# gate_w as SyncE's first transfer, and the gate's product on 16 partitions

## The chip, the core and the metric

One core of a Trainium2 chip runs the whole program. The metric is the device time of one execution in microseconds; a comparison takes the median of several runs. A profile is taken of one execution, and times within it count from the first instruction of the program (the span's start).

## The reference

A decode step for two rows x (2 x 1 x 512, bf16). Branch A is attention over a cache of 4096 keys and values for 32 heads of 128; branch B is a small ReLU network; a sigmoid gate mixes them.

```python
x = A_x                                                   # [2, 1, 512]
g = sigmoid((x * gate_w).sum(-1, keepdims=True))          # gate_w: [512]
q = (x @ wq).reshape(2, 1, 32, 128).transpose(0, 2, 1, 3)
s = einsum("bhqd,bhkd->bhqk", q, k_cache) * 128 ** -0.5   # k_cache: [2, 32, 4096, 128]
a = einsum("bhqk,bhkd->bhqd", softmax(s), v_cache)
a = a.transpose(0, 2, 1, 3).reshape(2, 1, 4096) @ wo
b = relu(x @ w1) @ w2                                     # w1: [512, 1376]
out = g * a + (1 - g) * b
```

The gate needs, for each of the two rows, one dot product of 512 elements; everything else hangs on reading the two caches, 67 MB each.

## The kernel before

The program is written as a list of instructions per engine with semaphores between them; each engine runs its list in order. SyncE's queue (sp) carries all large loads, in this order: wq (L218), w1 (L219), then sixteen units of 8 MB, eight of the K cache and eight of the V cache (L231; the last V unit in two parts, L226 and L228), then wo (L236) and w2 (L239 to L242), and at the end the output (L243). The order of the units is k0 to k4, then v0, k5, v1, k6, v2, k7, v3 to v7. They share three regions of SBUF (kv, three times 64 KB per partition). A unit is loaded when the unit three places earlier has been used up. wq and w1 lie in the third region, C, so the third unit, k2, waits for the q and h products and for the setup (L224). In the same region lie the small things of the beginning: x, gate_w, an identity and a block of ones.

ScalarE's queue carries two small loads: x as two rows of 1 KB (L216) and gate_w as one row of 1 KB (L217).

What the engines do in the first 20 us:

- GpSimd fills constants (constants(), L249 to L263).
- gate() (L280): TensorE transposes x to 128 partitions, four columns of two (L282, waits for x), and gate_w likewise (L285, waits for gate_w). VectorE copies the results out of PSUM (xT L287, a padded copy xT32 L289, gwT L291), multiplies x by gate_w on 128 partitions (L292), sums over the four columns (L294), and TensorE sums over the partitions with the block of ones (L296). ScalarE takes the exponential (L298); VectorE finishes the sigmoid after setup().
- setup() (L266): six small VectorE operations on the identity, masks for later. They stand in VectorE's list between the gate's sum and its sigmoid.
- q_proj() (L308): 32 products of TensorE (L313), which wait for wq and xT, then a VectorE transpose and a copy (L320, L323).
- ffn_h() (L327): 44 small products (L334), which wait for w1; VectorE applies ReLU and 1 - g (L338, L341).

Then, per K unit, VectorE transposes the unit in four pieces in place (k_turn, L358) and TensorE forms the scores (L363 and L391). A softmax runs per batch row (L397 to L420). Per V unit GpSimd spreads the probabilities (L429), TensorE multiplies (L446), VectorE extracts the diagonal blocks (L453, L457) and TensorE gathers them (L462). The end is project(): the products with wo and w2 (L499) into one PSUM tile, a copy (L505) and the output. The gate's value g is used first in the h branch (gm, 1 - g, L338) and then when the attention's result is scaled.

Of the kernel before, what the change touches and what calls it, by code (L numbers as in the profile page):

```python
# [4 lines left out]
ALU = mybir.AluOpType  # L5
ACT = mybir.ActivationFunctionType
AX = mybir.AxisListType
# [77 lines left out]
def bass_gated_mix__gqa_block_cached__dense_activation_relu__decode_kernel(  # L85
# [13 lines left out]
    bf16, f32 = dt.bfloat16, dt.float32  # L99

    sb = nc.alloc_sbuf_tensor
    kv = sb("kv", [128, NREG, REG], bf16)
# [5 lines left out]
    id2 = sb("id2", [2, 2], bf16)  # L108
    xT = sb("xT", [128, 4, 2], bf16)
    xT32 = sb("xT32", [128, 4, 32], bf16)  # L110
    gwT = sb("gwT", [128, 4], bf16)
    xg = sb("xg", [128, 4, 2], f32)
    xgs = sb("xgs", [128, 2], f32)
    ez = sb("ez", [128, 2], f32)
    ez1 = sb("ez1", [128, 2], f32)
    gb = sb("gb", [128, 2], f32)
# [23 lines left out]
    C = NREG - 1  # L140
    wq_sb = kv[:, C, 0:16384]
    w1_sb = kv[:, C, 16384:21888]
    x_sb = kv[0:2, C, 21888:22400]
    gw_sb = kv[0:1, C, 22400:22912]
    ident = kv[:, C, 22912:23168].bitcast(f32)
    ones = kv[:, C, 23168:23424].bitcast(f32)

    PSF = nc.alloc_psum_tensor("PS", [128, 4096], f32)
    PSB = PSF[:, :].bitcast(bf16)
# [6 lines left out]
    G_C0 = MISC + 64  # L156
    H_C0 = 7 * BANK + 400
    L_C0 = MISC + 96
    XT_B0 = 2 * (MISC + 400)

    def psf(p0, p1, c0, n):
        return PSF[p0:p1, c0:c0 + n]

    for e in ("pe", "dve", "act", "pool"):
        P.sems[e] = nc.alloc_semaphore(e + "_ev")
    names = ["x", "gw", "wq", "w1", "v7a", "v7b", "wo0", "wo1", "wo2", "w2a", "w2e", "w2b", "w2c", "w2d", "out"]
    sem = {n: nc.alloc_semaphore("sem_" + n) for n in names}
    sem_reg = [nc.alloc_semaphore(f"sem_reg{s}") for s in range(NREG)]

# [13 lines left out]
    def freed(what):  # L183
        kind, u = what
        return f"pe_sc_{u}" if kind == "k" else f"pe_v_{u}"

    def sp(fn, waits=(), dwaits=()):
        P.add("sp", fn, waits=waits, dwaits=dwaits)
# [4 lines left out]
    def dve(fn, waits=(), signal=None, dwaits=()):  # L193
        P.add("dve", fn, waits=waits, signal=signal, dwaits=dwaits)

    def act(fn, waits=(), signal=None, dwaits=()):
        P.add("act", fn, waits=waits, signal=signal, dwaits=dwaits)

    def pe(fn, waits=(), signal=None, dwaits=()):
        P.add("pe", fn, waits=waits, signal=signal, dwaits=dwaits)  # L200
# [13 lines left out]
    w2_sb = kv[:, WO, 16384:22016].rearrange("p (r n) -> p r n", n=512)  # L214

    act(lambda e: e.dma_start(x_sb, A_x.rearrange("b s d -> (b s) d")).then_inc(sem["x"], 16))  # L216
    act(lambda e: e.dma_start(gw_sb, gate_w.rearrange("(o d) -> o d", o=1)).then_inc(sem["gw"], 16))  # L217
    sp(lambda e: e.dma_start(wq_sb, A_wq.rearrange("(p t) n -> p (t n)", t=4)).then_inc(sem["wq"], 16))  # L218
    sp(lambda e: e.dma_start(w1_sb, B_w1.rearrange("(p t) f -> p (t f)", t=4)).then_inc(sem["w1"], 16))  # L219
    for n, what in enumerate(order):  # L220
        if n >= NREG:
            waits = [freed(order[n - NREG])]
        else:
            waits = ["pe_h", "dve_setup", "dve_q"] if n == C else []  # L224
# [5 lines left out]
        else:  # L230
            sp(lambda e, n=n, what=what: e.dma_start(kv[:, n % NREG, :], unit_in(what)).then_inc(sem_reg[n % NREG], 16),  # L231
               waits=waits)
# [8 lines left out]
    for name, r0, r1 in (("w2b", 0, 5), ("w2c", 5, 9), ("w2d", 9, 10)):  # L241
        sp(lambda e, name=name, r0=r0, r1=r1: e.dma_start(w2_sb[:, r0:r1, :], w2_in[:, r0:r1, :]).then_inc(sem[name], 16))  # L242
    sp(lambda e: e.dma_start(out.rearrange("b s (t n) -> t (b s) n", n=128), out_sb[0:128:16, :]).then_inc(sem["out"], 16),  # L243
       waits=["dve_out"])
# [21 lines left out]
    def setup():  # L266
        dve(lambda v: v.tensor_reduce(out=maskc[:], in_=ident.rearrange("p (t c h) -> p c t h", t=4, c=4), axis=AX.XY, op=ALU.add),
            waits=["c_ident"])
        dve(lambda v: v.tensor_reduce(out=mmax[:], in_=ident.rearrange("p (h x) -> p h x", h=8), axis=AX.X, op=ALU.add),
            signal="dve_m8")  # L270
        dve(lambda v: v.tensor_copy(out=mask8[:], in_=mmax[:]), waits=["dve_m8"], signal="dve_mask8")
        dve(lambda v: v.tensor_reduce(out=selx[:, 24:32], in_=ident.rearrange("p (y h) -> p h y", h=8), axis=AX.X, op=ALU.add),
            waits=["c_selx"], signal="dve_selx")
        for h in range(2):
            dve(lambda v, h=h: v.tensor_reduce(
                out=sell[:, h, :].rearrange("p (u a e) -> p e u a", u=4, a=4)[:, h],
                in_=ident.rearrange("p (a u r e) -> p e u a r", a=4, u=4, r=4)[:, h], axis=AX.X, op=ALU.add),
                waits=["c_sell"], signal=("dve_setup" if h == 1 else None))

    def gate():  # L280
        for t in range(4):
            pe(lambda e, t=t: e.transpose(PSB[0:128, XT_B0 + 2 * t:XT_B0 + 2 * t + 2], x_sb[:, t::4], id2[0:2, 0:2]),  # L282
               waits=(["c_id2"] if t == 0 else []), dwaits=([(sem["x"], 16)] if t == 0 else []))
        for t in range(4):
            pe(lambda e, t=t: e.transpose(PSB[0:128, XT_B0 + 8 + 2 * t:XT_B0 + 9 + 2 * t], gw_sb[:, t::4], id2[0:1, 0:1]),  # L285
               dwaits=([(sem["gw"], 16)] if t == 0 else []), signal=("pe_xT" if t == 3 else None))
        dve(lambda v: v.tensor_copy(out=xT[:], in_=PSB[0:128, XT_B0:XT_B0 + 8].rearrange("p (t b) -> p t b", t=4)),  # L287
            waits=["pe_xT"], signal="dve_xT0")
        dve(lambda v: v.tensor_copy(out=xT32[:, :, 0:2], in_=PSB[0:128, XT_B0:XT_B0 + 8].rearrange("p (t b) -> p t b", t=4)),  # L289
            waits=["c_x32"], signal="dve_x32")  # L290
        dve(lambda v: v.tensor_copy(out=gwT[:], in_=PSB[0:128, XT_B0 + 8:XT_B0 + 16:2]), signal="dve_xT")  # L291
        dve(lambda v: v.tensor_tensor(out=xg[:], in0=xT[:], in1=gwT[:].unsqueeze(2).to_broadcast([128, 4, 2]), op=ALU.mult),  # L292
            waits=["dve_xT"], signal="dve_xg")
        dve(lambda v: v.tensor_reduce(out=xgs[:], in_=xg[:].rearrange("p t b -> p b t"), axis=AX.X, op=ALU.add),  # L294
            waits=["dve_xg"], signal="dve_xgs")
        pe(lambda e: e.matmul(psf(0, 128, G_C0, 2), lhsT=ones, rhs=xgs[:, :], start=True, stop=True),  # L296
           waits=["dve_xgs", "c_ones"], signal="pe_z")
        act(lambda a: a.activation(out=ez[:], in_=psf(0, 128, G_C0, 2), func=ACT.Exp, scale=-1.0), waits=["pe_z"], signal="act_ez")  # L298
        setup()
        dve(lambda v: v.tensor_scalar(out=ez1[:], in0=ez[:], scalar1=1.0, scalar2=None, op0=ALU.add),  # L300
            waits=["act_ez"], signal="dve_ez1")
        dve(lambda v: v.reciprocal(out=gb[:], in_=ez1[:]), waits=["dve_ez1"], signal="dve_g")
        dve(lambda v: v.tensor_scalar(out=gm[:], in0=gb[:], scalar1=-1.0, scalar2=1.0, op0=ALU.mult, op1=ALU.add),
            waits=["dve_g"], signal="dve_gm")
# [202 lines left out]

    constants()
    gate()
    q_proj()  # L510
    w_block(0)
# [69 lines left out]
```

## Time and profile before

| | |
|---|---|
| median of 3 runs | 345.81 us (345.68 to 345.89) |
| the profiled execution, its own time | 345.56 us |
| its span | 344.24 us (344.2 on the page) |
| busy: TensorE products, VectorE, GpSimd, ScalarE | 53%, 49%, 10%, 4% of the span |
| SyncE's DMA queue, share of sixteen engines' time | 98.2% |
| read from HBM | 145.43 MB, 422 GB/s over the span |
| mean granted TensorE clock | 0.772 |
| x on TensorE, gate_w on TensorE, wq on TensorE | from 2.47, 7.99 and 13.14 us |

The page's slices cut the span into forty pieces of 8.6 us; a digit is the busy share in tenths. In a timeline line the first number is the start, the second the duration (from the first to the last instruction where several are merged), then engine, line of the kernel, operation, what is written and read, the count, and in brackets the idle time before with what ended it. A q behind an engine's name marks its sequencer issuing a DMA; the duration is that of the issue, not of the transfer. The packet records behind the DMA view hold, for each packet of a DMA engine, its start, duration, size and queue; q1 is SyncE's queue and q10 is ScalarE's.

### The profile page before, as it was taken

To read this page: it belongs to the slowest core of one execution; us is meant where nothing else is said; L and a number is where in the kernel's file an instruction comes from. 1 tells how busy PE (TensorE), PEld (TensorE's weight loads), DVE (VectorE), ACT (ScalarE), POOL (GpSimd) and SP (SyncE) were. 2 spreads that over 40 slices of the span, in tenths; PEclk is the share of its full clock that TensorE was granted. 3 is DMA by queue.
4 is the path that set the end of the run, shared out by engine and by line. 5 is a ranking of instruction groups with operands and counts; after the bars stand their busy time and mean duration, and the time that the engine had idled before them with its cause. 6 is when DMAs were issued, how large, how long until landed. Compare 5 with 4: busy or idle time off the path is not lost.

```text
span 344.2 us, 2542 instructions
## 1 busy us (share of the span) xinstructions
PE 182.1 (53%) x1322; PEld 40.5 (12%) x938; DVE 169.5 (49%) x86; ACT 12.9 (4%) x42; POOL 36.1 (10%) x50
## 2 busy tenths in 40 slices
PE   0520197996968409936970199206970604215453
PEld 0220000100100001110120002000120201102232
DVE  0210697979899489439810693119844010101020
ACT  1010001000010210100000000000020000000000
POOL 3000000000000040040022000400004040404000
PEclk9965579898999957995995589856995675856585
DMA  8998999999898999989899999999999999999994
GB/s 328 446 482 373 480 404 449 442 411 487 366 487 375 472 419 434 472 375 487 381 472 389 465 421 426 465 396 472 398 449 411 444 442 411 472 417 413 396 413 176
DMA packets 3744, 145.60 MB, mean 423 GB/s; under 512 B 434, under 2 KB 661, under 8 KB 917
## 3 DMA queue, kind: packets, MB, share of 16 engines
q1 hardware_dynamic: 3727, 145.43, 98.2%
q8 instruction: 9, 0.15, 0.2%
q14 instruction: 2, 0.02, 0.0%
q10 hardware_dynamic: 6, 0.00, 0.0%
HBM read 145.43 MB, written 0.00 MB: 422 GB/s over the span
## 4 chain that ended last, share of the span: by engine, by line
DMA 57%; DVE 20%; PE 13%; issue 4%; another core or an unknown queue 3%; SPq 1%; ACT 1%
DMA kv<-in_A_k_cache_dram 33%; DVE kv L358 18%; DMA kv<-in_B_w_dram 13%; DMA kv<-in_A_v_cache_dram 11%; PE PS L363 7%; PE PS L446 4%; PE PS L391 3%; DVE E L420 1%; ACT E L412 1%; DVE mpad L397 1%; SPq L236 0%; DVE X L457 0%; PE PS L499 0%; DVE X L453 0%
## 5 line engine op out<-in xcount | busy, mean ns | idle before, releaser
L358 DVE STREAM_TRANSPOSE kv<-kv 128x4096 uint32<-128x4096 uint32 x32 | 139.3, 4412 | 49.2 <-DMA kv<-in_A_k_cache_dram 49.2
L363 PE MATMUL PS<-kv,wz 128*128 128x512 bf16 x384 | 115.3, 411 | 0.0
L391 PE MATMUL PS<-kv,wz 128*128 128x512 bf16 x128 | 53.4, 417 | 92.3 <-DVE kv L358 92.3
L429 POOL TENSOR_TENSOR ptm<-E,mask 128x512 bf16<-128x512 bf16 x32 | 32.2, 1039 | 282.1 <-DVE E L420 158.6
L446 PE MATMUL PS<-kv,ptm 128*32 128x512 bf16 x512 | 38.4, 460 | 36.5 <-DMA kv<-in_A_v_cache_dram 36.5
L453 DVE TENSOR_TENSOR X<-PS,maskc 128x512 f32<-128x512 f32 x8 | 5.5, 686 | 79.3 <-PE PS L446 79.3
L391 PEld LDWEIGHTS PS<-kv,wz 128*128 128x128 bf16 x128 | 13.2, 103 | 205.0 <-DVE kv L358 116.6
L446 PEld LDWEIGHTS PS<-kv,ptm 128*32 128x32 bf16 x512 | 17.4, 113 | 54.4 <-issue 47.3
L349 ACT ACTIVATE wz<-q_sb 32x8 bf16<-32x8 bf16 x32 | 6.9, 215 | 154.2 <-PE PS L363 145.4
L462 PE MATMUL PS<-X,selx 128*32 128x128 f32 x16 | 3.5, 302 | 13.2 <-DVE X L457 13.2
L457 DVE TENSOR_REDUCE X<-X 128x128 f32<-128x512 f32 x8 | 8.2, 1024 | 0.3
L397 DVE TENSOR_REDUCE mpad<-PS 128x2 f32<-128x2048 f32 x2 | 4.6, 2292 | 7.5 <-PE PS L363 7.5
L412 ACT ACTIVATE E<-PS,negm 128x1024 bf16<-128x1024 f32 x4 | 4.4, 1108 | 81.9 <-DVE negm L408 81.9
L420 DVE STREAM_TRANSPOSE E<-E 128x2048 bf16<-128x2048 bf16 x2 | 4.6, 2311 | 4.7 <-ACT E L412 4.7
L313 PE MATMUL PS<-kv,xT 128*32 128x512 bf16 x32 | 3.6, 628 | 3.5 <-DMA kv<-in_A_wq_dram 3.5
L499 PE MATMUL PS<-kv,wz 128*17 128x128 bf16 x128 | 3.1, 264 | 3.8 <-DMA kv<-in_A_wo_dram 3.8
L505 DVE CAST ptm<-PS 128x128 bf16<-128x128 f32 x1 | 0.3, 292 | 9.5 <-PE PS L499 9.5
L320 DVE STREAM_TRANSPOSE ptm<-PS 128x1024 f32<-128x1024 f32 x1 | 1.2, 1250 | 6.2 <-PE PS L313 6.2
L287 DVE COPY xT<-PS 128x8 bf16<-128x8 bf16 x1 | 0.2, 162 | 8.3 <-PE PS L285 8.3
L462 PEld LDWEIGHTS PS<-X,selx 128*32 128x32 f32 x16 | 1.1, 112 | 18.9 <-DVE X L457 15.7
L285 PE MATMUL PS<-id,kv 1*128 1x1 bf16 x4 | 0.3, 172 | 5.3 <-DMA kv<-in_gate_w_dram 5.3
L499 PEld LDWEIGHTS PS<-kv,wz 128*17 128x17 bf16 x128 | 2.4, 109 | 4.3 <-DMA kv<-in_A_wo_dram 3.7
(57 smaller groups left out, 26.9 us busy)
## 6 DMA issues: line engine op xcount, KB each, us to landing
kv<-in_A_v_cache_dram SPq DMA_DIRECT2D x1, 6144.0 KB, 47.9
kv<-in_A_wq_dram SPq DMA_DIRECT2D x1, 4096.0 KB, 12.3
kv<-in_A_v_cache_dram SPq DMA_DIRECT2D x1, 2048.0 KB, 52.4
kv<-in_A_wo_dram SPq DMA_DIRECT2D x1, 2048.0 KB, 37.7
kv<-in_A_wo_dram SPq DMA_DIRECT2D x2, 1024.0 KB, 41.1
kv<-in_B_w_dram SPq DMA_DIRECT2D x1, 1376.0 KB, 15.1
kv<-in_B_w_dram SPq DMA_DIRECT2D x1, 640.0 KB, 42.9
kv<-in_B_w_dram SPq DMA_DIRECT2D x1, 512.0 KB, 43.7
```

What stands on the lines that cost most here:

```text
L349: act(lambda e, a=a: e.activation(out=wz[32 * a:32 * a + 32, u % 2, :, 31 + 32 * a:33 + 32 * a], in_=q_sb[32 * a:32 * a + 32, b, ub].rearr ...
L358: dve(lambda v, rp=rp: v.transpose(out=reg[:, 4096 * rp:4096 * (rp + 1)], in_=reg[:, 4096 * rp:4096 * (rp + 1)]), dwaits=([landed(what)] i ...
L363: return e.add_instruction(mybir.InstMatmult(name=nc.get_next_instruction_name(), engine=mybir.EngineType.PE, ins=[e.lower_ap(rhs), e.lowe ...
L391: return e.matmul(dst, lhsT=w, rhs=m, start=first, stop=final, skip_group_check=True)
L397: dve(lambda v: v.tensor_reduce(out=mpad[:, 0:2], in_=PSF[:, 0:2048].rearrange("p (x h q) -> p h x q", h=2, q=16), axis=AX.XY, op=ALU.max) ...
L412: act(lambda a, h=h: a.activation(out=E[:].rearrange("p (x h q) -> p h x q", h=2, q=16)[:, h], in_=PSF[:, 0:2048].rearrange("p (x h q) -> ...
L420: dve(lambda v: v.transpose(out=E[:], in_=E[:]), waits=[f"act_exp{b}"], signal=f"dve_et{b}")
L429: pool(lambda g, src=src, dst=dst: g.tensor_tensor(out=dst, in0=src, in1=msk, op=ALU.mult), waits=([f"dve_et{b}", "dve_mask8"] + ([f"pe_v_ ...
L446: pe(lambda e, ci=ci, t=t: e.matmul(psf(32 * t, 32 * t + 32, c0, 512), lhsT=ptm[:, ci].rearrange("p c h -> p (c h)"), rhs=rows[:, 512 * ci ...
L453: dve(lambda e: e.tensor_tensor(out=X2[:].rearrange("p (c d) -> p c d", c=4), in0=psf(0, 128, c0, 512).rearrange("p (c d) -> p c d", c=4), ...
L457: dve(lambda e: e.tensor_reduce(out=X3[:], in_=X2[:].rearrange("p (c d) -> p d c", c=4), axis=AX.X, op=ALU.add), waits=[f"dve_x_{v}"] + ([ ...
L499: pe(lambda e, t=t, n=n, w=w, m=m: e.matmul(psf(32 * t, 32 * t + 17, FIN_C0, 128), lhsT=w, rhs=m[:, 128 * t:128 * t + 128], start=(n == 0) ...
```

## The change

gate_w leaves ScalarE's queue and becomes the first transfer on SyncE's, ahead of wq, as 16 rows of 32 elements (64 bytes) on 16 partitions. ScalarE's second load becomes x16: x a second time, laid out on the same 16 partitions, 32 elements of each batch row on each. VectorE multiplies them there (16 partitions by 2 x 32) and sums over the 32; TensorE's sum with ones now runs over 16 partitions. The four transposes of gate_w and its copy out of PSUM are gone, and the transposes of x alone release the copies of x. The order of VectorE's list is otherwise kept. The new tiles lie in region C where gate_w's row was.

```diff
-    gwT = sb("gwT", [128, 4], bf16)
-    xg = sb("xg", [128, 4, 2], f32)
-    xgs = sb("xgs", [128, 2], f32)
+    xgs = sb("xgs", [16, 2], f32)
...
-    gw_sb = kv[0:1, C, 22400:22912]
+    x16 = kv[0:16, C, 22400:22464].rearrange("p (b c) -> p b c", b=2)
+    gw16 = kv[0:16, C, 22464:22496]
+    xg = kv[0:16, C, 22496:22624].bitcast(f32).rearrange("p (b c) -> p b c", b=2)
...
     act(lambda e: e.dma_start(x_sb, A_x.rearrange("b s d -> (b s) d")).then_inc(sem["x"], 16))
-    act(lambda e: e.dma_start(gw_sb, gate_w.rearrange("(o d) -> o d", o=1)).then_inc(sem["gw"], 16))
+    act(lambda e: e.dma_start(x16, A_x.rearrange("b s (r c) -> r (b s) c", c=32)).then_inc(sem["x16"], 16))
+    sp(lambda e: e.dma_start(gw16, gate_w.rearrange("(r c) -> r c", c=32)).then_inc(sem["gw"], 16))
     sp(lambda e: e.dma_start(wq_sb, A_wq.rearrange("(p t) n -> p (t n)", t=4)).then_inc(sem["wq"], 16))
     sp(lambda e: e.dma_start(w1_sb, B_w1.rearrange("(p t) f -> p (t f)", t=4)).then_inc(sem["w1"], 16))
...
     def gate():
         for t in range(4):
             pe(lambda e, t=t: e.transpose(PSB[0:128, XT_B0 + 2 * t:XT_B0 + 2 * t + 2], x_sb[:, t::4], id2[0:2, 0:2]),
-               waits=(["c_id2"] if t == 0 else []), dwaits=([(sem["x"], 16)] if t == 0 else []))
-        for t in range(4):
-            pe(lambda e, t=t: e.transpose(PSB[0:128, XT_B0 + 8 + 2 * t:XT_B0 + 9 + 2 * t], gw_sb[:, t::4], id2[0:1, 0:1]),
-               dwaits=([(sem["gw"], 16)] if t == 0 else []), signal=("pe_xT" if t == 3 else None))
+               waits=(["c_id2"] if t == 0 else []), dwaits=([(sem["x"], 16)] if t == 0 else []),
+               signal=("pe_xT" if t == 3 else None))
...
-        dve(lambda v: v.tensor_copy(out=gwT[:], in_=PSB[0:128, XT_B0 + 8:XT_B0 + 16:2]), signal="dve_xT")
-        dve(lambda v: v.tensor_tensor(out=xg[:], in0=xT[:], in1=gwT[:].unsqueeze(2).to_broadcast([128, 4, 2]), op=ALU.mult),
-            waits=["dve_xT"], signal="dve_xg")
-        dve(lambda v: v.tensor_reduce(out=xgs[:], in_=xg[:].rearrange("p t b -> p b t"), axis=AX.X, op=ALU.add),
-            waits=["dve_xg"], signal="dve_xgs")
-        pe(lambda e: e.matmul(psf(0, 128, G_C0, 2), lhsT=ones, rhs=xgs[:, :], start=True, stop=True),
+        dve(lambda v: v.tensor_tensor(out=xg, in0=x16, in1=gw16.unsqueeze(1).to_broadcast([16, 2, 32]), op=ALU.mult),
+            dwaits=[(sem["gw"], 16), (sem["x16"], 16)], signal="dve_xg")
+        dve(lambda v: v.tensor_reduce(out=xgs[:], in_=xg, axis=AX.X, op=ALU.add), waits=["dve_xg"], signal="dve_xgs")
+        pe(lambda e: e.matmul(psf(0, 128, G_C0, 2), lhsT=ones[0:16], rhs=xgs[:, :], start=True, stop=True),
            waits=["dve_xgs", "c_ones"], signal="pe_z")
```

More of the change, by code (lines that the diff above doesn't have):

```diff
@@ L165, in bass_gated_mix__gqa_block_cached__dense_activation_relu__decode_kernel @@
         P.sems[e] = nc.alloc_semaphore(e + "_ev")
-    names = ["x", "gw", "wq", "w1", "v7a", "v7b", "wo0", "wo1", "wo2", "w2a", "w2e", "w2b", "w2c", "w2d", "out"]
+    names = ["x", "gw", "x16", "wq", "w1", "v7a", "v7b", "wo0", "wo1", "wo2", "w2a", "w2e", "w2b", "w2c", "w2d", "out"]
     sem = {n: nc.alloc_semaphore("sem_" + n) for n in names}
```

## The prediction

> **What bounds the kernel now.** I read the page first, its slices and its queue table, then the DMA view of the stretch from 2 to 338 us, then the timeline at both ends, then the chain of waits and SyncE's own issues.
>
> From the page:
>
> ```profile
> span 344.2 us, 2542 instructions
> ...
> DMA  8998999999898999989899999999999999999994
> GB/s 328 446 482 373 480 404 449 442 411 487 366 487 375 472 419 434 472 375 487 381 472 389 465 421 426 465 396 472 398 449 411 444 442 411 472 417 413 396 413 176
> ...
> q1 hardware_dynamic: 3727, 145.43, 98.2%
> ```
>
> No compute engine is over 53% busy, but SyncE's queue (q1) fills 98.2% of the time of the sixteen DMA engines. The DMA view without the first 2 and the last 6 us:
>
> ```profile
> DMA packets 3421, 144.50 MB, mean 430 GB/s; under 512 B 380, under 2 KB 477, under 8 KB 608
> ...
> q1 hardware_dynamic: 3409, 144.36, 99.7%
> ```
>
> Between 2 and 338 us the engines are never without work. The trace's packet records say it more sharply: in every microsecond of that stretch more than 15 packets are in flight in the mean. So what the chain of waits names (33% K loads, 18% DVE transposes) is not the bound in the sense that a faster DVE would help: the loads are issued early enough. The time is: start of the stream, plus a fixed sum of packets, plus the tail behind the last one. The start and the tail:
>
> ```profile
> 0.73 0.54 ACTq L216 DMA_DIRECT2D kv<-in_A_x_dram  x1
> ...
> 0.74 0.39 SPq L218 DMA_DIRECT2D kv<-in_A_wq_dram  x1
> ...
> 1.18 0.42 SPq L219 DMA_DIRECT2D kv<-in_B_w_dram  x1
> 1.30 0.23 ACTq L217 DMA_DIRECT2D kv<-in_gate_w_dram  x1
> ...
> 2.47 0.26 PE L282 MATMUL PS<-id,kv 2*128 2x2 bf16 x4 [2.47 <-DMA kv<-in_A_x_dram]
> ...
> 7.99 0.29 PE L285 MATMUL PS<-id,kv 1*128 1x1 bf16 x4 [5.26 <-DMA kv<-in_gate_w_dram]
> ...
> 9.07 0.59 PE L296 MATMUL PS<-xgs,kv 128*128 128x2 f32 x2 [0.79 <-DVE xgs L294]
> ...
> 13.14 3.60 PE L313 MATMUL PS<-kv,xT 128*32 128x512 bf16 x32 [3.49 <-DMA kv<-in_A_wq_dram]
> ```
>
> ```profile
> 340.97 0.71 PE L499 MATMUL PS<-kv,hT 128*17 128x128 bf16 x20 [0.53 <-DMA kv<-in_B_w_dram]
> 341.73 0.29 DVE L505 CAST ptm<-PS 128x128 bf16<-128x128 f32 x1 [9.47 <-PE PS L499]
> 342.05 0.65 SPq L243 DMA_DIRECT2D out_dram<-ptm  x1
> ```
>
> To be seen here: SyncE's first instruction is the load of wq (0.74); by the packet records its first packet starts at 1.756, 1.02 us after the issue began. The last w2 packet ends at 340.80, and 0.71 + 0.29 + 0.65 us with small gaps and the output's way out follow. What happens on the compute engines at 3 to 13 us stands beside the stream.
>
> **The change, part by part.**
>
> *1. SyncE issues one more transfer ahead of wq.* SyncE starts at 0.74 as before, but with gate_w; wq, w1, k0 and k1 come one issue later. Rows for an issue on SyncE:
>
> ```profile
> 0.74 0.39 SPq L218 DMA_DIRECT2D kv<-in_A_wq_dram  x1
> ...
> 296.47 0.28 SPq L240 DMA_DIRECT2D kv<-in_B_w_dram  x1
> ```
>
> L240 has 8 rows (0.28), L218 128 rows (0.39), most loads of L231 (128 rows) take 0.33, and the first issue on ScalarE (L216, 2 rows) takes 0.54. Between issues lie 0.04 to 0.05. For 16 rows I take 0.33 + 0.05 = 0.38 us, with 0.28 + 0.04 = 0.32 and 0.54 + 0.05 = 0.59 as ends. Nothing hides it: until the first wq packet the engines are empty, and later there is no idle time to absorb it. **+0.38.**
>
> *2. More small packets.* Removed: gate_w as one row of 1 KB, which took 46 ns on one of the sixteen engines, with a 4-byte semaphore packet of 9. Added: 16 rows of 64 B on SyncE and 32 rows of 64 B (16 partitions, two batches) on ScalarE, plus their semaphore packets; spread evenly, an engine gets one and two rows. The gate_w row comes into an empty engine inside the 0.38 us just charged, so it costs nothing there; should wq start at once, it costs its own duration. No 64-byte packet is in the trace. Nearest are the 256-byte rows of the output, 15 to 18 ns, and the 1 KB rows in a busy stream, 46. For x16 I take 2 x 15 + 9 = 39 ns per engine, with 2 x 46 + 9 = 101 above and nothing below. **+0.04.** The far upper end is the first x packet, 1 KB in 366 ns; it is rival C.
>
> *3. wq's slow first packets.* The first packet of wq on each engine took 1.51 to 2.18 us, 1.885 in the mean, where later 32 KB packets take 1.213: 0.67 us per engine is lost. After the change a 64-byte row of gate_w comes first on each engine. If it uses up this cost, wq gets it back: between 0 and -0.67. The nearest rows: the first x packet took 366 ns where 1 KB otherwise takes 46, so about 0.32 is the price of an isolated read. But an isolated 16 KB instruction load at 340.9 us, when the engines have gone empty again, took 958 ns where 16 KB in the stream takes 612: 0.35 late in the program too. So it is more a price of each start from empty than a one-time one, and between gate_w (1.756 + 0.37 = 2.12) and wq (1.756 + 0.38 = 2.14) the engine runs empty again. I take **0**, by the 16 KB row, and keep -0.67 for the range.
>
> *4. The gate's arithmetic.* Four PE transposes (L285, 0.29 together) and one DVE copy (L291, 0.15) go; product and sum stay at one instruction each (0.17 and 0.16) and now wait for x16 and gate_w. The xT copy need no longer wait for gate_w: it moves from 8.32 to about 2.8. x16 takes the old place of gate_w on ScalarE's queue, and that row, issued at 1.30, reached an engine only at 6.35 (some four 32 KB packets of 1.21 stood ahead) and its semaphore packet another packet later, at 7.60. With two rows per engine I expect x16 at 8.8 to 10, so the DVE product starts up to 1.4 us later than the 8.65 of now. What is queued behind it: on DVE the setup reductions (1.2 us) and three small operations, done by about 12; on PE the L296 product, and behind it q_proj (L313), which waits for wq until 13.1 + 0.4 anyway. **0**, covered by wq's own landing with some 2 us to spare.
>
> *5. If that cover were gone.* A late q_proj would move L320 to L341 and the issue of k2 (it waits for the h product, setup and q; it went out at 19.4). But k2's first packets start only at 53.98, behind k0 and k1: 34 us of cover. Of the later loads v1 has least: issued 145.23, its packets begin at 150.71, 5.5 us of cover. All of these come from compute that follows landings, so they slide along with the stream and no new gap opens. DVE itself has room ahead of k0:
>
> ```profile
> 37.08 8.77 DVE L358 STREAM_TRANSPOSE kv<-kv 128x4096 uint32<-128x4096 uint32 x2 [17.07 <-DMA kv<-in_A_k_cache_dram]
> ```
>
> It stands idle for 17.07 us until k0 lands, then two of the transposes run; k0 lands later by what the stream is late.
>
> **Sum:** +0.38 + 0.04 + 0 + 0 = +0.42 us. The profiled execution took 345.56 us, 1.32 outside its span of 344.24; it becomes 344.66 and 345.98. The median of the runs shown is 345.81, 0.25 above the profiled one; the same step on it gives 346.23, which I round to **346.2 us** (+0.12%).
>
> **The rivals.**
>
> *A, the forecast (60%).* The stream starts one issue later and keeps its length. For it: the 98.2%, and no idle slice that could absorb a shift. With the ends of steps 1 and 2: 0.32 + 0 = +0.32 to 0.59 + 0.10 = +0.69, so 346.1 to 346.5.
>
> *B, the small transfer takes the cold start (25%).* gate_w's rows wake the engines, and wq's first packets run at 1.213. All 0.67 spared: 0.42 - 0.67 = -0.25, 345.56. Only the 0.32 that the first x packet lost: +0.10, 345.91, its likeliest value. For it: the loss is there in the first packets alone. Against: the 16 KB packet of 340.9 lost as much with nothing cold about it.
>
> *C, small rows hold their engine (12%), the slower side.* Each x16 row costs not 15 ns but an isolated read, 366, on every engine, in the middle of wq: 0.38 + 2 x 0.366 + 0.01 = +1.12, 346.9. It decides from about (0.69 - 0.38) / 2, 0.15 us per row. Against: gate_w's row of before sat between wq packets and took 46 ns, and the second x row 44; for: no row under 256 B has been seen, and 32 more come at once. The Trainium skill, "DMA: Bandwidth & Descriptors", section "Latency and other measured facts", says that a tiny transfer from HBM can't be quicker than a round trip of some 800 ns. Taken as time in which an engine is held, an estimate by that page is 1.756 + 0.8 = 2.56 for the end of gate_w (0.42 beyond wq's start) and 1.6 for x16, +2.4 in all, 348.2. The trace doesn't bear that out as held time: the isolated 1 KB row took 0.366 and the one in the stream 0.046.
>
> *D, the change doesn't make the gate earlier.* Quite possible, since x16 now waits where gate_w did; it changes no time (steps 4 and 5), so it has no share of its own.
>
> The remaining 3% are for what I don't see.
>
> **How the numbers follow.** A and B together are 85%; from B's -0.25 to A's +0.69 is 345.56 to 346.50. I widen the top to 346.65 for an issue and rows both at their upper ends with a little of C: 345.55 to 346.65. A difference under 0.2% (0.69 us) is about what a measurement of this kernel can't tell from no change; A and B lie within it. Slower by more: C's 12% less 2 for cheaper rows, A's upper edge 2, unseen 1: 0.13. Faster by more would need more than all of the 0.67 with a free issue: 0.02. Within: 0.85.
>
> **What would show it.** SyncE's timeline: gate_w at 0.74, wq at about 1.12, k0 at about 2.0. wq landing (start of L313) at 13.5 and the w2 landing (last L499) at 341.4: the same 0.4 at both ends is A. If L313 stays at 13.1, or wq's first packets take under 1.6 us, it is B. If wq's issue is 0.4 late and its landing over 0.8 late, it is C. The DMA share between 2 and 338 us should stay at 99.7% of q1. I am wrong in the frame if the stretch from k0 to the last w2 packet itself changes length, or if idle slices show up in the DMA row.

## The result and the profile after

The changed kernel takes **346.11 us** (median of 20 runs, 345.80 to 346.42), the kernel before 345.58 (20 runs, 345.24 to 345.89). The ratio is 1.0015, 95% interval 1.0009 to 1.0021: slower by 0.53 us (0.31 to 0.73), less than 0.2%, but clear of the scatter of that many runs. The forecast was +0.42 and 346.2.

The page of the changed kernel, the same rows as before:

```profile
span 344.9 us, 2535 instructions
...
DMA  7999989899998989899999999999999999999894
GB/s 305 467 456 395 486 367 479 372 479 448 403 486 367 479 380 471 380 465 471 395 471 389 456 397 456 464 403 464 395 450 410 448 450 395 479 408 446 370 413 166
...
q1 hardware_dynamic: 3759, 145.43, 98.0%
```

and its DMA view of 2 to 338 us:

```profile
DMA packets 3444, 144.74 MB, mean 431 GB/s; under 512 B 425, under 2 KB 521, under 8 KB 619
...
q1 hardware_dynamic: 3387, 144.60, 100.0%
```

The first digit of the DMA row went from 8 to 7; behind it some eights and nines change places, and no idle slice appears. The stream is as full as it was, with the same 145.43 MB. (q1 had 99.7% of the window before the change; twelve of wq's sixteen first packets started before 2 us there and lay outside it.) The timeline at the start:

```profile
0.74 0.40 SPq L218 DMA_DIRECT2D kv<-in_gate_w_dram  x1
...
1.20 0.41 SPq L219 DMA_DIRECT2D kv<-in_A_wq_dram  x1
1.31 0.33 ACTq L217 DMA_DIRECT2D kv<-in_A_x_dram  x1
...
2.48 0.16 DVE L286 COPY xT<-PS 128x8 bf16<-128x8 bf16 x1 [2.48 <-PE PS L283]
...
7.57 0.21 DVE L290 TENSOR_TENSOR kv<-kv 16x64 f32<-16x64 bf16 x1 [4.85 <-DMA kv<-in_A_x_dram]
...
9.46 0.17 DVE L300 TENSOR_SCALAR gm<-gb 128x2 f32<-128x2 f32 x1
...
13.62 3.61 PE L310 MATMUL PS<-kv,xT 128*32 128x512 bf16 x32 [4.95 <-DMA kv<-in_A_wq_dram]
```

and at the end:

```profile
341.56 0.71 PE L496 MATMUL PS<-kv,hT 128*17 128x128 bf16 x20 [0.53 <-DMA kv<-in_B_w_dram]
342.33 0.29 DVE L502 CAST ptm<-PS 128x128 bf16<-128x128 f32 x1 [9.57 <-PE PS L496]
342.64 0.65 SPq L244 DMA_DIRECT2D out_dram<-ptm  x1
```

wq is issued at 1.20 where it was 0.74, q_proj starts 0.48 later (13.62 against 13.14) and the last w2 products 0.59 later (341.56 against 340.97), although the gate itself is done a microsecond earlier (gm at 9.46 against 10.45). The packet records follow the delay through the program:

| | before | after | difference |
|---|---|---|---|
| wq issued | 0.74 | 1.20 | +0.46 |
| first packets of wq start, mean of 16 engines | 1.963 | 2.439 | +0.476 |
| their duration, mean | 1.885 | 1.914 | +0.03 |
| first 16 packets of k0 start, mean | 15.630 | 16.126 | +0.496 |
| last w2 packet ends | 340.796 | 341.355 | +0.559 |
| from k0's mean start to that end | 325.166 | 325.229 | +0.063 |

Of the 0.56 us at the end, 0.50 are there before K is touched, and 0.46 before the first packet of wq moves. Behind that, 325 us of program differ by 0.06 us. A single trace can't show this length much more sharply: over the nine kept traces, this section's two and the seven of the experiments, the same stretch lies between 324.83 and 325.27 us. What a change costs therefore rests on the medians below.

### The profile page after: what moved, and what is told of

Its sections match the earlier page's. It is cut to its first block, busy times and chain, and to the rows that moved or that the text cites. A ratio compares the mean times of both kernels' runs of the same rounds, so it can differ in the third digit from the quotient of the medians.

```text
span 344.9 us, 2535 instructions
## 1 busy us (share of the span) xinstructions
PE 179.2 (52%) x1318; PEld 40.1 (12%) x934; DVE 169.5 (49%) x85; ACT 12.9 (4%) x42; POOL 36.1 (10%) x50
## 3 DMA queue, kind: packets, MB, share of 16 engines
q1 hardware_dynamic: 3759, 145.43, 98.0%
HBM read 145.43 MB, written 0.00 MB: 422 GB/s over the span
## 4 chain that ended last, share of the span: by engine, by line
DMA 57%; DVE 24%; PE 9%; issue 4%; another core or an unknown queue 3%; SPq 1%; ACT 1%
DMA kv<-in_A_k_cache_dram 33%; DVE kv L355 21%; DMA kv<-in_B_w_dram 13%; DMA kv<-in_A_v_cache_dram 11%; PE PS L360 4%; PE PS L443 4%; PE PS L388 2%; DVE E L417 1%; ACT E L409 1%; DVE mpad L394 1%; SPq L237 0%; DVE X L454 0%; PE PS L496 0%; DVE X L450 0%
## 5 line engine op out<-in xcount | busy, mean ns | idle before, releaser
L360 PE MATMUL PS<-kv,wz 128*128 128x512 bf16 x384 | 113.0, 404 | 0.0
L388 PE MATMUL PS<-kv,wz 128*128 128x512 bf16 x128 | 52.5, 410 | 94.7 <-DVE kv L355 94.7
```

The lines of the kernel that those rows point to most:

```text
L360: return e.add_instruction(mybir.InstMatmult(name=nc.get_next_instruction_name(), engine=mybir.EngineType.PE, ins=[e.lower_ap(rhs), e.lowe ...
L388: return e.matmul(dst, lhsT=w, rhs=m, start=first, stop=final, skip_group_check=True)
```

## The experiments

Two theories were tried against each other. **Issue theory:** the time is what SyncE's first issue takes, because nothing behind it has idle time to give. **Row theory:** the 48 rows of 64 bytes cost the stream time wherever they are issued (rival C in small). Rival B, the spared cold start, was out with the second and third row of the table above. Every run is compared with the kernel before on the same chip.

**e1: gate_w's rows back on ScalarE's queue.**

```diff
-    sp(lambda e: e.dma_start(gw16, gate_w.rearrange("(r c) -> r c", c=32)).then_inc(sem["gw"], 16))
+    act(lambda e: e.dma_start(gw16, gate_w.rearrange("(r c) -> r c", c=32)).then_inc(sem["gw"], 16))
```

> The changed kernel with one thing undone: gate_w's 16 rows go back to ScalarE's queue, behind x16, so that wq is SyncE's first transfer again. Rows, 16 partitions and arithmetic stay as changed. Issue theory (the time is what SyncE's first issue takes, 0.46 us): wq's issue back at 0.74, its first packet at 1.76, L313's counterpart back at 13.1, and the time is that of before, ratio 0.9997 to 1.0004. Row theory (the 48 small rows cost the stream its time wherever they are issued): the 0.5 us stays, ratio 1.0012 to 1.0020. Either way the gate's product comes later, at about 10 us, since gate_w now waits behind x16 and wq packets.

Measured: 345.50 us against 345.54, ratio 1.0000 (0.9991 to 1.0008). The time is back, with all 48 rows and the new arithmetic in place. Its timeline:

```profile
0.73 0.38 SPq L219 DMA_DIRECT2D kv<-in_A_wq_dram  x1
...
1.67 0.43 ACTq L218 DMA_DIRECT2D kv<-in_gate_w_dram  x1
...
11.65 0.21 DVE L290 TENSOR_TENSOR kv<-kv 16x64 f32<-16x64 bf16 x1 [8.95 <-DMA kv<-in_gate_w_dram]
```

wq is first again (0.73), and the gate's product comes at 11.65, 4.1 us later than in the changed kernel (expected: about 10), which costs nothing.

**e2: the move alone, in the kernel before.**

```diff
-    act(lambda e: e.dma_start(gw_sb, gate_w.rearrange("(o d) -> o d", o=1)).then_inc(sem["gw"], 16))
+    sp(lambda e: e.dma_start(gw_sb, gate_w.rearrange("(o d) -> o d", o=1)).then_inc(sem["gw"], 16))
```

> The kernel before with one part of the change alone: gate_w, still as one row of 1 KB and with the old transposes, is SyncE's first transfer. Issue theory: an issue of 0.25 to 0.40 us and a gap of 0.05 stand ahead of wq, so the first wq packet comes at 2.05 to 2.25 and the time rises by 0.3 to 0.5 us, ratio 1.0009 to 1.0015; if an issue of one row is shorter than one of 16 (0.23 against 0.40 on the two queues), it is the lower end. Row theory: no row was cut and none added, ratio 0.9997 to 1.0004.

Measured: 345.89 against 345.54, ratio 1.0010 (1.0001 to 1.0018).

```profile
0.73 0.35 SPq L217 DMA_DIRECT2D kv<-in_gate_w_dram  x1
...
1.14 0.36 SPq L218 DMA_DIRECT2D kv<-in_A_wq_dram  x1
```

One row of 1 KB, no small row anywhere, and the time rises with the issue: wq goes out at 1.14, 0.40 late, and the median is 0.35 up. An issue of one row takes 0.35 here, one of 16 rows 0.40: the count of rows hardly matters.

**e3: two transfers ahead of wq.** gate_w and x16 both on SyncE, in this order.

```diff
-    act(lambda e: e.dma_start(x16, A_x.rearrange("b s (r c) -> r (b s) c", c=32)).then_inc(sem["x16"], 16))
     sp(lambda e: e.dma_start(gw16, gate_w.rearrange("(r c) -> r c", c=32)).then_inc(sem["gw"], 16))
+    sp(lambda e: e.dma_start(x16, A_x.rearrange("b s (r c) -> r (b s) c", c=32)).then_inc(sem["x16"], 16))
```

> The changed kernel with x16 moved as well: gate_w and then x16 are SyncE's first two transfers, ScalarE loads x alone. Same rows, same arithmetic as changed. Issue theory: two issues ahead of wq, wq issued at about 1.6, first packet at 2.6 to 2.7, and the time is 0.85 to 1.0 us above before, ratio 1.0024 to 1.0030. Row theory: as the changed kernel or a little less, since x16's rows now run while the engines are still empty, ratio 1.0010 to 1.0016. The gate's product should come early, by 3 us, and be worth nothing.

Measured: 346.51 against 345.54, ratio 1.0027 (1.0017 to 1.0038).

```profile
0.73 0.39 SPq L217 DMA_DIRECT2D kv<-in_gate_w_dram  x1
...
1.19 0.41 SPq L218 DMA_DIRECT2D kv<-in_A_x_dram  x1
...
1.64 0.42 SPq L219 DMA_DIRECT2D kv<-in_A_wq_dram  x1
...
4.73 0.17 DVE L300 TENSOR_SCALAR gm<-gb 128x2 f32<-128x2 f32 x1
```

Twice the dose, twice the price: wq 0.90 late, the median 0.97 up. The gate is done at 4.73, earlier than in any other of these kernels, and this is the slowest of them.

**e4: gate_w behind wq.**

```diff
-    sp(lambda e: e.dma_start(gw16, gate_w.rearrange("(r c) -> r c", c=32)).then_inc(sem["gw"], 16))
     sp(lambda e: e.dma_start(wq_sb, A_wq.rearrange("(p t) n -> p (t n)", t=4)).then_inc(sem["wq"], 16))
+    sp(lambda e: e.dma_start(gw16, gate_w.rearrange("(r c) -> r c", c=32)).then_inc(sem["gw"], 16))
```

> The changed kernel with gate_w's 16 rows on SyncE's queue but behind wq instead of ahead of it. Issue theory: wq starts at 0.74 as before, and gate_w's issue of 0.4 is covered, because wq's packets last until 12 us and w1 and k0 are issued long before their turn: ratio 0.9997 to 1.0004. Row theory: as the changed kernel, 1.0012 to 1.0020. The gate then waits for gate_w until wq has landed, so the gate's product moves to about 13 us and q_proj, behind it on TensorE, from 13.1 to about 14; this should cost nothing, as k2's packets start only at 54.

Measured: 345.44 against 345.54, ratio 0.9997 (0.9988 to 1.0006).

```profile
0.74 0.39 SPq L218 DMA_DIRECT2D kv<-in_A_wq_dram  x1
...
1.18 0.42 SPq L219 DMA_DIRECT2D kv<-in_gate_w_dram  x1
...
13.28 0.21 DVE L290 TENSOR_TENSOR kv<-kv 16x64 f32<-16x64 bf16 x1 [10.56 <-DMA kv<-in_gate_w_dram]
...
14.30 1.47 PE L310 MATMUL PS<-kv,xT 128*32 128x512 bf16 x12
...
15.17 0.17 DVE L300 TENSOR_SCALAR gm<-gb 128x2 f32<-128x2 f32 x1
```

The same issue of 0.42 us, on the same queue, one place later, costs nothing that can be measured. The gate is later than in the kernels above (15.17) and even delays q_proj to 14.30, and still the time is that of before.

**e5: eight more loads of x16.** The kernel of e1 and, on ScalarE's queue behind gate_w, eight loads that nothing uses; k2's issue waits for them as well.

```diff
+    for i in range(8):
+        xx = kv[0:16, C, 23424 + 64 * i:23488 + 64 * i].rearrange("p (b c) -> p b c", b=2)
+        act(lambda e, xx=xx: e.dma_start(xx, A_x.rearrange("b s (r c) -> r (b s) c", c=32)).then_inc(sem["xx"], 16))
```

> The kernel of e1_gw_on_act with eight more loads of x16 (32 rows of 64 bytes each, into unused columns of region C) on ScalarE's queue behind gate_w; k2 waits for them too. The output doesn't use them. It prices small rows in the middle of the stream. By the packet records an engine gets per load two rows of 8 to 11 ns and a semaphore packet of 9, 28 ns, eight times 0.22 us: ratio 1.0003 to 1.0010 to before, time 0.1 to 0.35 above e1. If a small row held its engine for an isolated read (0.366 us), eight loads would cost 8 x 0.73 = 5.9 us, ratio 1.017.

Measured: 346.40 against 345.56, ratio 1.0022 (1.0014 to 1.0031).

```profile
2.14 4.09 ACTq L221 DMA_DIRECT2D kv<-in_A_x_dram  x8
```

Neither number was met. 0.84 us for 256 rows, 16 per engine, is 0.05 us per row with its share of a semaphore packet: far from the 0.366 of rival C, but more than the packets' own durations (16 x 11 + 8 x 9 ns = 0.25 us per engine). The excess stands in the median alone. In the profiled run, the quickest of its eleven, the last w2 packet ends 0.34 us later than e1's, not much more than those durations, and the slower runs left no trace. One other thing differs in e5: since k2 waits for the extra loads, it is issued at 47.21 instead of 19.38, 7 us before its packets start. In the profiled run no DMA engine stands idle there; for the other runs it can't be ruled out. So whether the rows cost more than they are busy, and why, stays open. For the change e5 bounds x16's two rows per engine: 0.03 us by their durations, 0.1 by this median.

**e6: w1 ahead of wq**, the two lines swapped in the kernel before.

> The kernel before with wq and w1 swapped on SyncE's queue, nothing else: the first packet of each engine has 11 KB in place of 32 KB. It asks whether the 0.67 us that each engine loses in its first packet belongs to wq's large rows or to any start. If to any start (as the changed kernel suggests, where gate_w's rows went first and wq's first packets still took 1.91 us): w1's first packets take 0.413 + 0.6 to 0.7, wq's 1.213, time as before, ratio 0.9995 to 1.0005. If it belongs to the size or to wq: up to 0.6 us gained, ratio 0.9982 to 0.9990.

Measured: 345.66 against 345.56, ratio 1.0002 (0.9993 to 1.0011).

```profile
0.74 0.39 SPq L218 DMA_DIRECT2D kv<-in_B_w_dram  x1
...
1.18 0.42 SPq L219 DMA_DIRECT2D kv<-in_A_wq_dram  x1
...
16.32 3.60 PE L313 MATMUL PS<-kv,xT 128*32 128x512 bf16 x32 [8.21 <-DMA kv<-in_A_wq_dram]
```

By the packet records w1's first packets took 0.974 us in the mean, where its others take 0.413, and wq's took 1.213 like any later one. The loss, 0.56, went with the place and not with wq. q_proj starts 3.2 us later than before (16.32), which again costs nothing.

**e7: w1 as ScalarE's first transfer**, ahead of x, instead of SyncE's second.

```diff
+    act(lambda e: e.dma_start(w1_sb, B_w1.rearrange("(p t) f -> p (t f)", t=4)).then_inc(sem["w1"], 16))
     act(lambda e: e.dma_start(x_sb, A_x.rearrange("b s d -> (b s) d")).then_inc(sem["x"], 16))
...
-    sp(lambda e: e.dma_start(w1_sb, B_w1.rearrange("(p t) f -> p (t f)", t=4)).then_inc(sem["w1"], 16))
```

> The kernel before with w1 as ScalarE's first transfer, ahead of x and gate_w, while SyncE's first stays wq: each engine is offered packets of two queues at the start, and SyncE issues one transfer less ahead of k0. If the start loss is an engine's waiting for its first read, two queues fill it and up to 0.4 us (a w1 packet's 0.413) is gained, ratio 0.9985 to 0.9993. If the loss is the same for all packets at the start, the time is that of before, ratio 0.9995 to 1.0005. SyncE's saved issue is worth nothing in either case, as it stands behind wq. x and gate_w come later, at some 13 us, and q_proj with them, which k2's cover of 34 us hides.

Measured: 345.75 against 345.56, ratio 1.0004 (0.9995 to 1.0013).

```profile
0.73 0.40 ACTq L216 DMA_DIRECT2D kv<-in_B_w_dram  x1
...
0.73 0.38 SPq L219 DMA_DIRECT2D kv<-in_A_wq_dram  x1
```

No gain. Though both queues were issued at 0.73, the first w1 packet started at 3.556, when the first wq packets (1.91 us in the mean) began to end: the second queue did not fill the loss. x and gate_w came later than the 13 us expected: x reaches TensorE at 20.74 and gate_w at 25.53, q_proj starts at 27.12, the gate is done at 27.99 and k2 is issued at 33.50. That costs nothing measurable either: k2's first packets start at 54.31 in the mean, before at 54.37.

No version beats the kernel before; e1 and e4 keep the new arithmetic at its time. The five that bear on the two theories, side by side:

| kernel | wq issued, later than before | first 16 packets of k0, later | time, above before | gate done at |
|---|---|---|---|---|
| e4 | 0.00 | 0.04 | -0.10 | 15.17 |
| e1 | -0.01 | -0.03 | -0.04 | 13.55 |
| e2 | 0.40 | 0.39 | +0.35 | 4.82 |
| changed | 0.46 | 0.50 | +0.53 | 9.46 |
| e3 | 0.90 | 0.93 | +0.97 | 4.73 |

The time follows the second and third columns and has nothing to do with the last. From the start of wq's issue to its first packet it is 1.02 us before the change, 1.04 after, 0.99 in e2 and 1.04 in e3: what stands ahead of wq shifts its start and adds nothing else.

## Why the prediction was right, step by step

*The frame.* A stream without idle time, so that its start passes to its end: shown by the dose (0.40, 0.46, 0.90 us of issue gave 0.35, 0.53, 0.97), with the same delays already in k0's first packets. The Trainium skill, "DMA: Bandwidth & Descriptors", section "Issuing engines are not separate DMA queues", says that another issuing engine saves only the sequencer's time to start a DMA, which is usually small beside the transfer. The trace agrees that this time is what is at stake: 0.46 us of the 0.53. It is small beside wq, whose packets run for 10.9 us, but not beside gate_w, whose packets run for 0.17.

*Step 1, +0.38.* The largest term, a little small: issue 0.40 and gap 0.06, so 0.46. I had taken the duration of later 128-row loads (0.33); the first issue on the queue, wq's own 0.39 before the change, was the nearer row. e2 shows that the rows' number adds 0.05 at most.

*Step 2, +0.04.* gate_w's 16 packets ran from 1.751 to 1.93, in the empty time ahead of wq, free as assumed. x16's rows took 8 and 11 ns and its semaphore packet 9, 28 ns per engine. e1 says that with all rows in place nothing is lost to within 0.3 us, and e5 puts x16 at about 0.1 by its median. So the term is not contradicted, and too small to be measured alone. What the 0.53 holds beyond 0.46, 0.07 us, lies within the scatter, and I don't assign it.

*Step 3, 0.* The number is shown, but its reason was not: wq's first packets took 1.885 us before and 1.914 after small packets had gone through every engine, 1.855 to 1.930 in e1 to e4. e6 shows that the loss belongs to whatever large packet comes first. Rival B falls. But the row that decided for 0 was misread. The isolated instruction load of 16 KB (958 ns) was set against SyncE's 16 KB packets (612 ns); the eight other instruction loads of that size in the same trace, inside the full stream, took 1.015 to 1.099 us, so the isolated one lost nothing. The 366 ns of the first x packet don't come again either: in the seven other traces in which x is ScalarE's first load, its two rows took 44 to 126 ns. A price of each start from empty is therefore not shown, and that 0 came true was luck in this respect. Why the first large packet is slow stays open.

*Step 4, 0.* Right in its cost, wrong in its course. I let x16 arrive at 8.8 to 10 us, later than gate_w had, because I let it wait as gate_w's row had, behind three wq packets by the packet records (the prediction says some four). Where wq is issued first, this holds: x16's last semaphore packet ends at 8.85 in e1 and 9.12 in e4. In the changed kernel wq itself starts 0.48 us later, and x16 met only wq's first packet: its rows run from 4.115 and the last semaphore packet ends at 7.12. The gate came 1.0 us earlier, not 1.4 later. No time hung on it.

*Step 5, the covers.* They held where they were tried: q_proj at 14.30 (e4), at 16.32 (e6) and at 27.12 (e7) cost nothing measurable.

*Rival C.* Not in the changed kernel: no 64-byte packet took over 11 ns, and C's price per row, 0.366 us, came from the one packet that no other trace repeats (step 3). The 800 ns of the Trainium skill, "DMA: Bandwidth & Descriptors", section "Latency and other measured facts", for a tiny transfer isn't borne out as time that an engine is held. e5 leaves 0.05 us a row by its median, a seventh of C's price.

*The base.* 346.2 was 345.81 plus 0.42; the median of 20 runs of before is 345.58, 0.23 lower than that of the three shown, and the step was 0.11 larger than forecast. These two partly offset each other, so part of the closeness of 346.2 to 346.11 is luck. The prediction took a difference under 0.2% for about what can't be told from none; with 20 runs of each kernel, 0.53 us could be told.

## What to carry to other kernels

Where the DMA queue is full from its first packet to its last, look at what the issuing engine does before that first packet: in this kernel each issue ahead of the first large load cost its whole 0.4 us, and the same issue one place later, or on the other queue, cost nothing measurable. To get a small operand earlier is worth something only if a wait on it ends last somewhere; here the gate moved between 4.7 and 28 us without any effect of its own. A first transfer that was small did not spare the large one behind it its slow start. And before a slow packet is put down to its place, compare it with others of its own queue and size, and look for it in a second trace.

## What was not expected of the hardware

- An issue on SyncE takes nearly the same for one row of 1 KB (0.35 us), 16 rows of 64 B (0.40) and 128 rows of 32 KB (0.36 to 0.42).
- The first large packet on each engine loses 0.56 us (11 KB, e6) or 0.64 to 0.75 (32 KB, e1 and e5), after small packets as well, and offering a second queue at the same moment changed nothing (e7).
- ScalarE's small rows come one per turn between SyncE's packets: in the changed kernel an engine's two x16 rows and the semaphore packet stand 1.22 us apart (first ones at 4.115, 5.333 and 6.550), a 32 KB packet between them. So x16, three small packets per engine, landed two large packets after its first row.
- With sixteen more 64-byte rows per engine in a full stream the median rose by 0.84 us (1.4 to 3.1 thousandths), about three times their own durations; where the rest goes wasn't found, and the one trace kept shows 0.34.
